# Splitting two table loads and moving the issue of the first feed-forward weights and of the inverse tables

## Chip, core and metric

The kernel runs on one core of a Trainium2 chip. The metric is the device time of one execution in microseconds (us): the median of several runs, with a profile taken of one further execution. Five engines work side by side, each through its own list of instructions in order: PE (matmuls), DVE and ACT (elementwise work, and moving results out of PSUM, the matmul accumulators), POOL, and SP (SyncE), which here only issues DMA transfers. PEld is PE's loading of stationary operands. The transfers of SP and of POOL run on the same 16 DMA engines.

## What is computed

A token mixer in the frequency domain, then a feed-forward block, each after a layer norm and with a residual. S is 2048, D is 576, F is 4608, all in bf16.

```python
def _A_ref(x, w_r, w_i):
    X = rfft2(x.astype(float32), axes=(-2, -1))
    X = X * (w_r + 1j * w_i)
    return irfft2(X, s=(S, D), axes=(-2, -1)).astype(bfloat16)

def _B_ref(x, w_gate, w_up, w_down):
    return (_gelu(x @ w_gate) * (x @ w_up)) @ w_down

x = A_x
h = x + _A_ref(_layernorm(x), A_w_r, A_w_i)
h2 = h + _B_ref(_layernorm(h), B_w_gate, B_w_up, B_w_down)
```

## The kernel before

The 2048 rows are held as 16 chunks of 128. The transforms are matmuls with constant tables that lie in DRAM and are loaded by DMA. The work goes through four stages.

1. **First layer norm and transform** (to about 20 us). Chunks of x and the table ATAB are loaded, the rows are scaled, and matmuls of line 551 give the tile U.
2. **Filter stage** (about 20 to 44 us). It runs over 16 groups of frequencies, numbered 0 to 15 in the order of GORD (group index 1 to 15, then 0). For each group there are five kinds of step. `D` (line 640) transforms along D with the table FT, its two halves written `D` and `d`, and is evicted to CUS. `B` (line 660) is a forward transform of 16 points with the table BT, evicted to YS. `T` (line 673, on DVE) multiplies by the filter weights WS. `V` and `v` (line 681) are the two halves of the inverse 16-point transform of the first 256 columns, with the table VT, evicted to V. `R` and `r` (line 698) do the same for the last 32 columns of four groups at once, with VT too; their result RB is scattered to VR by small DMAs (line 242, the helper that issues every DMA).
3. **Inverse stage** (about 44 to 57 us). `I`, `i` (line 830, with the table DT) and `N`, `o` (line 847, with the table IT) finish the inverse transform of eight of the chunks. `E` evicts to GS, `a` adds the residual, `s`, `q`, `c`, `n` are the second layer norm, `u` and `U` (line 899, with the unit matrix IDT) turn the normed rows, and `e` evicts them to the tile HT. The other eight chunks are done later, between the first feed-forward matmuls, with the tables DP and ITD (from about 63 us).
4. **Feed-forward** (from 57 us to the end). `G0` and `G1` are its first matmuls (line 939): G0 covers the first 256 of the first 512 rows, G1 the others. They use weight slot 0 of the tile WG. Line 1039 is the down projection.

The order inside the filter and the inverse stage is written out by hand, in the strings `SEQF` and `SEQ`. The part of `SEQF` around the first steps of `V` and `R` reads

```python
... d8 D7 T3 B4 d7 V0 D6 v0 V1 T5 d6 v1 R0 V2 r0 v2 T4 ...
```

Semaphore waits are derived from names: an operation lists what it reads and writes, and the engine that issues it waits for the last writers. A DMA is issued in the order of the program on its engine. Where SP must not issue a DMA too early, `hold()` makes SP wait for the last PE operation emitted so far.

Two lists of loads matter here. The first is issued by SP at the start with no waits: x and ATAB, FT (432 KB), BT (128 KB), the first half of the filter weights WS (groups 1 to 8), VT (384 KB), the second half of WS, and the two small rows of group 0 (`w_zero`). Once the weights are there, half of WS is copied to the other partitions, by POOL, DVE and POOL's DMAs (`dup_w`).

The second is the dictionary `LOADS`. Its keys are steps of `SEQF`, or of `SEQ` with a dot in front. After that step is emitted, the loads named in its value are: `0` to `9` are ten pieces of the first feed-forward weights (`wg0_part`, gate and up columns 0 to 1151 into slot 0 of WG, eight of 288 KB and two of 144 KB, each behind a `hold()`), `t` is `tab_load` (DT, IT and the unit matrix, behind a wait for the last copy of WS), and `d` is `tab2_load` (DP and ITD, behind a `hold()`). Piece 9 completes the tile; the matmuls of line 939 wait for all ten.

BT holds two tables of 64 KB: `BT[:, 0]` serves the fifteen groups with nonzero index, `BT[:, 1]` group index 0, which comes last (B15). VT holds six of 64 KB: `VT[:, 0]` serves the `V` steps of the fifteen groups, 1 and 2 those of group index 0 (V15), 3 to 5 the `R` steps.

Of the kernel before, what the change touches and what calls it, by code (L numbers as in the profile page):

```python
# [27 lines left out]
SEQF = """D2 D0 d2 D1 d0 d1 B2 D5 B0 d5 T2 D3 B1 d3 D4 T0 T1 B5 d4 D8 B3 d8 D7 T3 B4 d7 V0 D6 v0 V1 T5 d6 v1 R0 V2 r0 v2 T4 B6 D9 B8 T6 V3 d9 D11 v3 d11 B7 D10 B9 d10 V6 V4 T7 v6 v4 V5 B10 v5 R1 D12 T8 r1 d12 B11 T9 V7 D14 v7 T10 d14 D13 B12 d13 D15 T11 V9 T12 d15 v9 V8 B13 v8 R2 r2 T13 B14 T14 B15 V12 V10 v12 v10 V13 V11 T15 v13 V14 v11 v14 V15 R3 v15 r3""".split()  # L28
VENG = [('act',), ('act', 'dve'), ('act', 'dve'), ('act', 'dve'), ('act', 'dve'), ('dve',), ('act', 'dve'), ('act', 'dve'), ('dve',), ('act', 'dve'), ('act',), ('dve',), ('act',), ('act', 'dve'), ('act',), ('act', 'dve')]
DENG, BENG = ['act', 'dve', 'act', 'act', 'act', 'act', 'act', 'act', 'dve', 'act', 'act', 'act', 'act', 'act', 'act', 'act'], ['act', 'dve', 'act', 'act', 'act', 'act', 'act', 'dve', 'act', 'act', 'act', 'act', 'act', 'act', 'act', 'act']  # L30
LOADS = {"r0": "t", "v12": "0", "v15": "1", ".I0": "2", ".i1": "3", ".N0": "4", ".i3": "5", ".o1": "6", ".N3": "7", ".o3": "8 9", ".i7": "d"}
RENG = ['dve', 'act', 'act', 'act', 'act']
QR = ((0, 1), (1, 2), (2, 3), (3, 4), (4, 8), (8, 16))
DEF0, DSTEP = 3, 4
# [3 lines left out]
def _np_bf16(a):  # L38
    npdt = mybir.dt.np(BF16)
    return np.ascontiguousarray(np.asarray(a, dtype=np.float32).astype(npdt))  # L40
# [291 lines left out]
def _build(nc, A_x, A_w_r, A_w_i, B_w_gate, B_w_up, B_w_down, out):  # L332
    P = Prog(nc)
    T = build_tables()
    dram = {n: nc.inline_tensor(_np_bf16(T[n]), name="c_" + n.lower()) for n in T}
    PE, DVE, ACT, SP, POOL = "pe", "dve", "act", "sp", "pool"
# [51 lines left out]
    FT = sb.alloc("FT", [128, 6, 2 * HK], BF16)  # L388
    BT = sb.alloc("BT", [128, 2, 2, 128], BF16)
    VT = sb.alloc("VT", [128, 6, 2, 128], BF16)  # L390
# [20 lines left out]
    TR = sb.alloc("TR", [128, 2, 2, 2, 128], BF16)  # L411
# [9 lines left out]
    PS = nc.alloc_psum_tensor("PS", [128, 4096], F32)  # L421

    def bank(b, p0=0, p1=128, c0=0, c1=512):
        return PS[p0:p1, b * 512 + c0:b * 512 + c1]

    def banks(b, n, w):
        return PS[:, b * 512:(b + n) * 512].rearrange("p (a c) -> p a c", a=n)[:, :, 0:w]
# [16 lines left out]
    for i, w in enumerate(LORD):  # L444
        (x_load if w[0] == "x" else atb_load)(i, int(w[1:].split("-")[0]), int(w.split("-")[1]))
    P.dma(SP, FT[:, :, :].rearrange("p a b -> p (a b)"), dram["FTAB"][:, :], "ft", w=["FT"])
    P.dma(SP, BT[:, :, :, :].rearrange("p a b c -> p (a b c)"), dram["BTAB"][:, :], "bt", w=["BT"])

    def w_up(pl, hf):
        g0, g1 = ((0, 9), (9, 16))[hf]  # L450
# [5 lines left out]
    def w_down(pl, hf, sls=(0, 1, 2, 3), eng=SP, sem=""):  # L456
        g0, g1 = ((1, 9), (9, 16))[hf]
        src = (A_w_r, A_w_i)[pl].tensor
        for sl in sls:
            p0 = 64 * (sl // 2) + 32  # L460
            P.dma(eng, WS[p0 + sl % 2:p0 + 32:2, sl // 2, pl, g0:g1, :], bass.AP(src, (64 + 16 * (3 - sl) + 16 - g0) * K2, [[128 * K2, 16], [-K2, g1 - g0], [1, K2]]),
                  f"w{pl}{hf}{sem}", w=[("W", hf, pl, 2 + sl)])

    def w_zero(pl):
        for jp in range(2):
            P.dma(SP, WS[64 * jp + 32:64 * jp + 64, jp, pl, 0, :], bass.AP((A_w_r, A_w_i)[pl].tensor, (64 + 32 * jp) * K2, [[128 * K2, 16], [(-16 if jp else 48) * K2, 2], [1, K2]]),
                  f"wz{pl}", w=[("W", 2, pl, jp)])

    for pl in (1, 0):
        w_up(pl, 0)  # L470
        w_down(pl, 0)
    P.dma(SP, VT[:, :, :, :].rearrange("p a b c -> p (a b c)"), dram["VTAB"][:, :], "vt", w=["VT"])
    for pl in (1, 0):
        w_up(pl, 1)
        w_down(pl, 1, (0, 1, 2, 3) if pl else (0, 1))
    for pl in (1, 0):
        w_zero(pl)
    GORD = list(range(1, NG)) + [0]
    wkeys = [[("W", hf, pl, h) for pl in range(2) for h in range(6 if hf < 2 else 2)] for hf in range(3)]

# [100 lines left out]
    for w in SEQ1:  # L581
        a = w[1:]
# [9 lines left out]
    for t, w in enumerate(SEQF):  # L592
        k, i = w[0], w[1:].rstrip("abc")
        if k in "DBVR":
            b = min((b for b in used if b not in busy), key=lambda b: used[b])
# [4 lines left out]
        elif k in "dvr":  # L600
            b = FB[k.upper(), int(i)]
# [3 lines left out]
    def ev(eng, dst, src, r, w):  # L605
        fn = (lambda v: v.tensor_copy(dst, src)) if eng == DVE else (lambda a: a.activation(dst, src, ACTF.Copy))  # L606
        P.op(eng, fn, r=r, w=w)
# [47 lines left out]
    def st_B(i, eng=ACT):  # L655
        sl, s3, sp_ = i % NY, i % 3, 1 if GORD[i] == 0 else 0
        b0 = FB["B", i]
        for m in range(2):
            for h in range(2):
                P.op(PE, lambda t, m=m, h=h: t.matmul(bank(b0 + h, 0, 128, 0, KW), BT[64 * h:64 * h + 64, sp_, m, :], CUS[64 * h:64 * h + 64, s3, m, :], start=(m == 0), stop=(m == 1)),  # L660
                     r=[("CU", s3), "BT"], w=[("PS", b0 + h)])
        ev(eng, YS[:, sl, :, :], banks(b0, 2, KW), [("PS", b0), ("PS", b0 + 1)], [("Y", sl)])

    def st_T(i, hs=(0, 1)):
        g, sl, z = GORD[i], i % NY, i % NZ
        q, j = i // 4 % 2, i % 4
# [9 lines left out]
    def st_V(i, second, engs):  # L676
        g, z, b0 = GORD[i], i % NZ, FB["V", i]

        def mm(h, o, ct, first, last, after):
            c, t_ = ct  # L680
            return P.op(PE, lambda t: t.matmul(bank(b0 + o, 0, 128, 128 * c, 128 * c + 128), TP[64 * h:64 * h + 64, z, o, t_, c:256:2], VT[64 * h:64 * h + 64, 0 if g else 1 + o, t_, :],  # L681
                                               start=first, stop=last), r=[("T", z), "VT"], w=[("PS", b0 + o)], after=after)

        halves(("V", i), second, [[(c, t_) for c in range(2) for t_ in range(2)]] * 2, mm)
        if not second:
            return
        v5 = V[:, :, :, :, g, :, :].rearrange("p c t n j e -> p j (c t n) e")
        n = 2 // len(engs)
        for a, e in enumerate(engs):
            ev(e, v5[:, n * a:n * a + n], banks(b0 + a, n, 256).rearrange("p a (c e) -> p a c e", e=4), [("PS", b0 + a + k) for k in range(n)], [("V", g, a + k) for k in range(n)])  # L690

    def st_R(q, second):
        js = range(4 * q, 4 * q + 4)
        b0 = FB["R", q]

        def mm(h, o, pt, first, last, after):
            part, t_ = pt
            return P.op(PE, lambda t: t.matmul(bank(b0 + o, 0, 128, 128 * part, 128 * part + 128), TR[64 * h:64 * h + 64, q % 2, o, t_, :], VT[64 * h:64 * h + 64, 4 + o if part else 3, t_, :], start=first, stop=last),  # L698
                        r=[("TR", q % 2, j) for j in range(4)] + ["VT"], w=[("PS", b0 + o)], after=after)

        halves(("R", q), second, [[(part, t_) for part in range(1 + (q == 3)) for t_ in range(2)]] * 2, mm)
        if not second:
            return
        keys = [("PS", b0), ("PS", b0 + 1)]
        if q < 3:
            ev(RENG[q], RB[:, q, :, :, :, :].rearrange("p t o e n -> p o t (e n)"), banks(b0, 2, 128).rearrange("p o (t x) -> p o t x", t=2), keys, [("RB", q)])
            for j, i in enumerate(js):
                for t_ in range(2):
                    k = (2 * j + t_) % 3 > 0
                    P.dma((SP, POOL)[k], VR[64 * t_ + 32 * (j % 2):64 * t_ + 32 * (j % 2) + 32, GORD[i], :, :, :], RB[32 * j:32 * j + 32, q, t_, :, :, :], f"r{q}{k:d}", r=[("RB", q)], w=[("V", GORD[i], 2 + t_)])  # L710
            return
        for i in js:
            j, g = i % 4, GORD[i]
            for t_ in range(2):
                dst = VR[64 * t_ + 32 * (j % 2):64 * t_ + 32 * (j % 2) + 32, g, :, :, :].rearrange("p o e n -> p o (e n)")
                src = PS[32 * j:32 * j + 32, b0 * 512:(b0 + 2) * 512].rearrange("p (a c) -> p a c", a=2)[:, :, 128 * (i == LAST) + 64 * t_:128 * (i == LAST) + 64 * t_ + 64]
                ev((ACT, DVE, DVE, ACT)[j], dst, src, keys, [("V", g, 2 + t_)])
# [21 lines left out]
    c = 0  # L739
    while c < NT:  # L740
        c1 = c + 1
        while c not in ACT_TILES and c1 < NT and c1 not in ACT_TILES:
# [3 lines left out]
             r=[(keys, k) for k in range(c, c1)], w=[("NM", k) for k in range(c, c1)])  # L746
        c = c1
    for k in (2, 3):
        for jp in range(2):
            last = dup_w(k, jp)  # L750
# [22 lines left out]
    def loads(w):  # L773
        for v in LOADS.get(w, "").split():
            (tab_load if v == "t" else tab2_load if v == "d" else lambda: wg0_part(int(v)))()

    for w in SEQF:
        i = int(w[1:].rstrip("abc"))
# [14 lines left out]


    P.alias(sum(wkeys, []) + sum(dup, []), [("WG", j, k) for j in (1, 2) for k in range(4)])
    P.alias(["FT", "BT", "VT"], [("HT", 0, i, k) for i in range(4) for k in range(5)])

    vmain = [("V", g, c) for g in range(NG) for c in range(2)]
    vtail = [("V", g, c) for g in range(NG) for c in range(2, 4)]
# [4 lines left out]
    SLOT, last, held, ing = {}, [sorted(used.values()).index(used[2 * b]) - 4 for b in range(4)], set(), False  # L804
    for t, w in enumerate(SEQ):
        k, i = w[0], int(w[1:].rstrip("ADSP"))
        if k in "INu":
            b = min((b for b in range(2 * ing, 4) if b not in held), key=lambda b: last[b])
# [3 lines left out]
        elif k in "ioUEae":  # L812
            b = SLOT[{"i": "I", "o": "N", "U": "u", "E": "I", "a": "N", "e": "u"}[k], i] // 2
# [145 lines left out]
    for w in SEQ:  # L959
        a = w[1:]  # L960
# [96 lines left out]
    for tb in range(4):  # L1057
# [26 lines left out]
        for w in "0 1 0 2 1 3 2 3".split() if tb < 3 else "0 1 0 2 1 2".split():  # L1084
            first = ("Z", tb, int(w)) not in ends
# [39 lines left out]
```

## Time and profile before

| what | value |
| --- | --- |
| median of 3 runs | 489.72 us (488.74 to 489.88) |
| profiled execution | 487.7 us, span of its instructions 485.9 us |
| granted TensorE clock | 1.00 |
| PE busy | 476.7 us, 98% of the span |
| DVE, ACT, POOL busy | 182.9, 146.6, 52.8 us |
| chain that ended last | PE 93%, DMA 1% |
| matmuls of line 939 with slot WG | 2142, 233.3 us busy |
| DMA moved | 33.19 MB, 68 GB/s over the span |

The profile is that of one execution on the chip. Times in its rows are microseconds from the start of the span. A timeline row gives start, duration, engine, line, operation, what is written and read, and in brackets how long the engine stood idle before it and what ended that. A row of waits gives the engine and line that waited, what it waited for, and then the total in us, the number of times and the longest. A windows row gives the stretch, its length, the busy time of the engine with its instruction count, the granted clock, the mean busy share of the 16 DMA engines (which can pass 1 where transfers overlap in one engine), and GB/s. SP's own instructions appear as SPq.

### The profile page before, as it was taken

Reading aid. Unit: us, or ns where it says so; the run is one execution under the profiler, and the core shown is the slowest. Engines: PE = TensorE matmul, PEld = TensorE weight load, DVE = VectorE, ACT = ScalarE, POOL = GpSimd, SP = SyncE. Lnnn points to the kernel's source line nnn. Section 1 sums busy time; section 2 is a strip of 40 time slices with the busy share of each in tenths; the row PEclk is TensorE's granted clock in tenths of the full one; section 3 lists DMA queues with packets and bytes.
Section 4 is the critical chain, followed back from the end, with each engine's and each line's share of the span. In section 5 each row is a group of like instructions: output and inputs, shape, how many; then the busy total and the mean of one; then the engine's idle time right before and its main releaser. Section 6 shows DMA issues by size and latency. Waiting matters only on the chain.

```text
span 485.9 us, 12883 instructions
## 1 busy us (share of the span) xinstructions
PE 476.7 (98%) x5872; PEld 279.4 (57%) x5872; DVE 182.9 (38%) x366; ACT 146.6 (30%) x295; POOL 52.8 (11%) x88
## 2 busy tenths in 40 slices
PE   7899899999999999999999999999999999999998
PEld 3777665544477744444577644444777444444774
DVE  7898756566501133333200233333101233333011
ACT  6998664443400023322200023322100133223000
POOL 6873317010120000000000000000000000000000
PEclk9999999999999999999999999999999999999999
DMA  8965598941440001100000011000000000000000
GB/s 287 210 161 177 175 306 285 377 110 24 131 143 26 27 15 20 23 0 1 1 15 15 26 21 23 14 2 1 3 13 26 14 1 0 1 1 1 3 26 26
DMA packets 26966, 33.19 MB, mean 68 GB/s; under 512 B 12560, under 2 KB 19104, under 8 KB 26912
## 3 DMA queue, kind: packets, MB, share of 16 engines
q1 hardware_dynamic: 23248, 19.87, 14.7%
q0 software_dynamic: 3664, 12.50, 8.0%
q8 instruction: 46, 0.75, 0.7%
q14 instruction: 8, 0.07, 0.0%
HBM read 26.21 MB, written 2.36 MB: 59 GB/s over the span
## 4 chain that ended last, share of the span: by engine, by line
PE 93%; DMA 1%; DVE 0%; issue 0%; SPq 0%; DVEq 0%
PE PS L939 58%; PE PS L1039 27%; PE PS L1051 2%; PE PS L640 2%; PE PS L681 2%; DMA WG<-in_B_w_up_dram 1%; PE PS L830 1%; PE PS L660 1%; PE PS L989 1%; PE PS L847 1%; PE PS L1006 0%; PE PS L698 0%; DVE CUS L606 0%; DVE V L606 0%; SPq L242 0%
## 5 line engine op out<-in xcount | busy, mean ns | idle before, releaser
L939 PE MATMUL PS<-HT,WG 64*128 64x512 bf16 (+1 forms) x2142 | 233.3, 372 | 1.2 <-DMA WG<-in_B_w_up_dram 1.2
L939 PEld LDWEIGHTS PS<-HT,WG 64*128 64x128 bf16 x2142 | 105.2, 94 | 116.1 <-DMA WG<-in_B_w_up_dram 1.3
L947 ACT ACTIVATE GL<-PS 128x512 bf16<-128x512 f32 x144 | 85.7, 596 | 282.9 <-PE PS L939 282.9
L948 DVE TENSOR_TENSOR AT<-GL,PS 128x512 bf16<-128x512 bf16 x144 | 98.8, 687 | 167.1 <-ACT GL L947 167.1
L1039 PE MATMUL PS<-WD,AT 64*128 64x288 bf16 x2160 | 132.9, 283 | 0.0
L1039 PEld LDWEIGHTS PS<-WD,AT 64*128 64x128 bf16 x2160 | 103.3, 94 | 29.8
L1026 DVE TENSOR_TENSOR OS<-PS,XO 128x288 bf16<-128x288 f32 (+2 forms) x32 | 13.3, 453 | 125.5 <-PE PS L1039 118.0
L939 PE MATMUL PS<-HT,WGX 64*128 64x512 bf16 x486 | 53.4, 376 | 0.0
L939 PEld LDWEIGHTS PS<-HT,WGX 64*128 64x128 bf16 x486 | 23.2, 94 | 29.2
L856 ACT ACTIVATE OS<-XO,NM 128x576 bf16<-128x576 bf16 x15 | 11.6, 774 | 11.4 <-DVE XO L1010 11.4
L640 PE MATMUL PS<-FT,U 64*128 64x288 bf16 x160 | 13.5, 284 | 0.3 <-DVE CUS L606 0.3
L673 DVE TENSOR_TENSOR TP<-YS,WS 128x1024 bf16<-128x1024 bf16 x16 | 11.0, 688 | 0.5 <-DMA WS<-WS 0.5
L551 PE MATMUL PS<-ATS,XO 128*128 128x128 bf16 x96 | 8.2, 219 | 3.0 <-POOL ATS L520 2.1
L494 DVE BATCH_NORM_STATS2 ST<-XO 128x6 f32<-128x288 bf16 x26 | 9.9, 441 | 2.1 <-DMA XO<-in_A_x_dram 2.0
L562 ACT ACTIVATE U<-PS 128x384 bf16<-128x384 f32 (+2 forms) x31 | 10.4, 419 | 1.1 <-PE PS L551 0.9
L681 PE MATMUL PS<-VT,TP 64*128 64x128 bf16 x256 | 10.0, 217 | 0.0
L242 POOL DMA_DIRECT2D WG<-in_B_w_gate_dram x9 | 6.1, 678 | 35.1 <-DMA WG<-in_B_w_gate_dram 30.6
L551 PEld LDWEIGHTS PS<-ATS,XO 128*128 128x128 bf16 x96 | 6.9, 98 | 4.4 <-POOL ATS L520 2.9
L242 POOL DMA_DIRECT2D WD<-in_B_w_down_dram x9 | 6.7, 755 | 24.4 <-PE PS L1006 24.4
L606 ACT ACTIVATE CUS<-PS 128x576 bf16<-128x576 f32 x14 | 9.0, 653 | 0.8 <-PE PS L640 0.7
L1051 PE MATMUL PS<-WD,AT 128*128 128x448 bf16 (+1 forms) x72 | 9.0, 286 | 0.0
L606 ACT ACTIVATE YS<-PS 128x576 bf16<-128x576 f32 x14 | 8.8, 653 | 0.2
(88 smaller groups left out, 229.5 us busy)
## 6 DMA issues: line engine op xcount, KB each, us to landing
WD<-in_B_w_down_dram POOLq DMA_DIRECT2D x9, 576.0 KB, 10.6
WG<-in_B_w_up_dram SPq DMA_DIRECT2D x6, 576.0 KB, 6.8
WG<-in_B_w_gate_dram POOLq DMA_DIRECT2D x6, 576.0 KB, 5.8
out_dram<-OS SPq DMA_DIRECT2D x30, 72.0 KB, 1.7
XO<-in_A_x_dram SPq DMA_DIRECT2D x3, 576.0 KB, 7.5
WG<-in_B_w_gate_dram SPq DMA_DIRECT2D x4, 288.0 KB, 3.8
WG<-in_B_w_up_dram SPq DMA_DIRECT2D x4, 288.0 KB, 3.6
WGX<-in_B_w_up_dram SPq DMA_DIRECT2D x2, 576.0 KB, 4.6
```

The lines of the kernel that those rows point to most:

```text
L242: fn = lambda e: e.dma_start(out_ap, in_ap)
L551: P.op(PE, lambda t, b=b, lhs=lhs, p0=p0, p1=p1, s=s, e=e, o=o, c=c: t.matmul(bank(b, p0, p1, o, o + 128), lhs, ATS[:, c, :], start=s, sto ...
L606: fn = (lambda v: v.tensor_copy(dst, src)) if eng == DVE else (lambda a: a.activation(dst, src, ACTF.Copy))
L640: return P.op(PE, lambda t: t.matmul(bank(b0 + o, 0, 128, 0, 2 * HK), U[64 * h:64 * h + 64, us, 2 * i:2 * i + 2, :, :], FT[64 * h:64 * h + ...
L681: return P.op(PE, lambda t: t.matmul(bank(b0 + o, 0, 128, 128 * c, 128 * c + 128), TP[64 * h:64 * h + 64, z, o, t_, c:256:2], VT[64 * h:64 ...
L856: P.op(ACT, lambda a, c=c, out=out: a.activation(out, XO[:, c, 0:D], ACTF.Square, bias=NM[:, c:c + 1], accum_out=SB2[:, 1, c:c + 1]), r=[( ...
L939: op = P.op(PE, lambda t, h0=h0, kt=kt, wt=wt, b=b, s=(not second and j == 0), e=(second and j == n - 1): t.matmul(bank(b, 0, 128, c0, c1) ...
L947: P.op(ACT, lambda a: a.activation(GL[:, s2, :], bank(b0), ACTF.Gelu_apprx_tanh), r=[("PS", b0)], w=[("GL", s2)])
L948: P.op(DVE, lambda v: v.tensor_tensor(AT[:, f, :], GL[:, s2, :], bank(b0 + 1), op=ALU.mult), r=[("GL", s2), ("PS", b0 + 1)], w=[("AT", f)])
L1026: P.op(DVE, lambda v: v.tensor_tensor(OS[:, p % 2, d0:d1], bank(b, 0, 128, 0, d1 - d0), XO[:, c, d0:d1], op=ALU.add), r=[("PS", b), ("X", ...
L1039: e[h] = P.op(PE, lambda t, f=f, h=h, r0=r0, j=j: t.matmul(bank(b0 + h, 0, 128, 0, 288), AT[r0:r0 + 64, f, 128 * p:128 * p + 128], WD[r0:r ...
L1051: P.op(PE, lambda t, b=b, d0=d0, d1=d1, f=f, j=j: t.matmul(bank(b, 0, 128, 0, d1 - d0), AT[:, f, 128 * p:128 * p + 128], WD[:, f, d0:d1], ...
```

## The change

Three things are changed, and no computation.

- The loads of the two 16-point tables are each made in two parts. `BT[:, 0]` and `VT[:, 0]` (64 KB each) stay where the whole table was loaded. `VT[:, 1:6]` (320 KB) and `BT[:, 1]` (64 KB) are issued after the last of the filter weights, under the names VT2 and BT2. B15 now waits for BT2, and V15 and all `R` steps for VT2.
- The ten weight pieces are attached to other steps: 0 and 1 to d7, 2 to v9, 3 to v8, 4 to v12, 5 to v13, 6 to v15, 7 to I0, 8 and 9 to i1. Before, the first was attached to v12 and the last to o3 of the inverse stage.
- `tab_load` moves from r0 to r1, and `tab2_load` from i7 to N1.

```diff
-LOADS = {"r0": "t", "v12": "0", "v15": "1", ".I0": "2", ".i1": "3", ".N0": "4", ".i3": "5", ".o1": "6", ".N3": "7", ".o3": "8 9", ".i7": "d"}
+LOADS = {"d7": "0 1", "r1": "t", "v9": "2", "v8": "3", "v12": "4", "v13": "5", "v15": "6", ".I0": "7", ".i1": "8 9", ".N1": "d"}
...
-    P.dma(SP, BT[:, :, :, :].rearrange("p a b c -> p (a b c)"), dram["BTAB"][:, :], "bt", w=["BT"])
+    P.dma(SP, BT[:, 0, :, :].rearrange("p b c -> p (b c)"), dram["BTAB"][:, 0:256], "bt", w=["BT"])
...
-    P.dma(SP, VT[:, :, :, :].rearrange("p a b c -> p (a b c)"), dram["VTAB"][:, :], "vt", w=["VT"])
+    P.dma(SP, VT[:, 0, :, :].rearrange("p b c -> p (b c)"), dram["VTAB"][:, 0:256], "vt", w=["VT"])
     for pl in (1, 0):
         w_up(pl, 1)
         w_down(pl, 1, (0, 1, 2, 3) if pl else (0, 1))
     for pl in (1, 0):
         w_zero(pl)
+    P.dma(SP, VT[:, 1:6, :, :].rearrange("p a b c -> p (a b c)"), dram["VTAB"][:, 256:1536], "vt2", w=["VT2"])
+    P.dma(SP, BT[:, 1, :, :].rearrange("p b c -> p (b c)"), dram["BTAB"][:, 256:512], "bt2", w=["BT2"])
...
 st_B:  r=[("CU", s3), "BT2" if sp_ else "BT"]
 st_V:  r=[("T", z), "VT" if g else "VT2"]
 st_R:  r=[("TR", q % 2, j) for j in range(4)] + ["VT2"]
```

The last three lines give only what the reading side of each step now names.

More of the change, by code (lines that the diff above doesn't have):

```diff
@@ L660, in st_B @@
                 P.op(PE, lambda t, m=m, h=h: t.matmul(bank(b0 + h, 0, 128, 0, KW), BT[64 * h:64 * h + 64, sp_, m, :], CUS[64 * h:64 * h + 64, s3, m, :], start=(m == 0), stop=(m == 1)),
-                     r=[("CU", s3), "BT"], w=[("PS", b0 + h)])
+                     r=[("CU", s3), "BT2" if sp_ else "BT"], w=[("PS", b0 + h)])
         ev(eng, YS[:, sl, :, :], banks(b0, 2, KW), [("PS", b0), ("PS", b0 + 1)], [("Y", sl)])
@@ L681, in mm @@
             return P.op(PE, lambda t: t.matmul(bank(b0 + o, 0, 128, 128 * c, 128 * c + 128), TP[64 * h:64 * h + 64, z, o, t_, c:256:2], VT[64 * h:64 * h + 64, 0 if g else 1 + o, t_, :],
-                                               start=first, stop=last), r=[("T", z), "VT"], w=[("PS", b0 + o)], after=after)
+                                               start=first, stop=last), r=[("T", z), "VT" if g else "VT2"], w=[("PS", b0 + o)], after=after)
         halves(("V", i), second, [[(c, t_) for c in range(2) for t_ in range(2)]] * 2, mm)
@@ L698, in mm @@
             return P.op(PE, lambda t: t.matmul(bank(b0 + o, 0, 128, 128 * part, 128 * part + 128), TR[64 * h:64 * h + 64, q % 2, o, t_, :], VT[64 * h:64 * h + 64, 4 + o if part else 3, t_, :], start=first, stop=last),
-                        r=[("TR", q % 2, j) for j in range(4)] + ["VT"], w=[("PS", b0 + o)], after=after)
+                        r=[("TR", q % 2, j) for j in range(4)] + ["VT2"], w=[("PS", b0 + o)], after=after)
         halves(("R", q), second, [[(part, t_) for part in range(1 + (q == 3)) for t_ in range(2)]] * 2, mm)
@@ L795, in _build @@
     P.alias(sum(wkeys, []) + sum(dup, []), [("WG", j, k) for j in (1, 2) for k in range(4)])
-    P.alias(["FT", "BT", "VT"], [("HT", 0, i, k) for i in range(4) for k in range(5)])
+    P.alias(["FT", "BT", "VT", "BT2", "VT2"], [("HT", 0, i, k) for i in range(4) for k in range(5)])
     vmain = [("V", g, c) for g in range(NG) for c in range(2)]
```

## The prediction

> **What bounds the kernel now.** I read the page first: PE is busy 476.7 of the 485.9 us of the span and the chain of waits gives it 93%. So the change can only matter where PE stands still between 20 us, where the tables of the change are first used, and the first feed-forward matmul. The view of PE's waits from 20 to 57.5 us has four rows in all:
>
> ```profile
> PE PS L939 <- DMA WG<-in_B_w_up_dram: 1.2, 1, 1.2
> PE PS L830 <- DVE V L606: 0.4, 1, 0.4
> PE PS L640 <- DVE CUS L606: 0.3, 1, 0.3
> PE PS L830 <- DVE XO L853: 0.2, 1, 0.2
> ```
>
> That is 2.1 us to be had. The first row is the last of the ten weight pieces. The chain of waits up to 60 us, and SyncE's part of the timeline, show how it comes about:
>
> ```profile
> 51.15 0.37 PE PS L830 x6
> 51.52 0.27 PE PS L847 x4
> 51.78 0.39 SPq L242
> 52.17 0.04 issue
> 52.22 4.96 DMA WG<-in_B_w_up_dram
> 57.17 0.05 issue
> 57.22 2.79 PE PS L939 x47
> ```
>
> ```profile
> 14.05 0.59 SPq L242 DMA_DIRECT2D VT<-c_vtab  x1
> ...
> 22.96 1.36 SPq L242 DMA_DIRECT2D WS<-in_A_w_r_dram  x2
> 30.20 2.65 SPq L242 DMA_DIRECT2D VR<-RB  x3
> 37.55 0.33 SPq L242 DMA_DIRECT2D DT<-c_dtab  x1
> ...
> 43.43 0.58 SPq L242 DMA_DIRECT2D WG<-in_B_w_gate_dram  x1
> ...
> 52.22 0.60 SPq L242 DMA_DIRECT2D WG<-in_B_w_up_dram  x1
> ```
>
> The reader is to see that the pieces start only at 43.43, that the last is issued at 52.22 because it is held to an inverse matmul that ends at 51.78, and that it lands 4.96 us later, since the pieces and the deferred tables keep the transfer engines about 0.9 busy from 45 to 55 us. Meanwhile the stretches from 27 us on stand almost empty. The windows by microsecond (PE busy, clock, DMA share, GB/s) read:
>
> ```profile
> 25.00:26.00 1.00, 1.00 (x20) 1.00 0.88 213
> 26.00:27.00 1.00, 1.00 (x20) 1.00 0.74 198
> 27.00:28.00 1.00, 1.00 (x27) 1.00 0.21 59
> 28.00:29.00 1.00, 1.00 (x36) 1.00 0.04 10
> 29.00:30.00 1.00, 1.00 (x34) 1.00 0.00 0
> ```
>
> **Part 1, the weight pieces.** The change issues the same ten DMAs, only earlier. Their holds now end, by the places of these steps in PE's chain: d7 at 27.5 us (pieces 0 and 1), v9 and v8 at 39.2 and 39.9 (2, 3), v12, v13 and v15 between 41.6 and 44.0 (4, 5, 6), I0 at 44.8 (7), i1 at about 46.5 (8, 9). The last piece is therefore issued by about 47.4, and with the slowest landing of such a piece here (4.96 us) it is there at 52.4, some 3.7 us before it can be used. What is late next at G0, line 939? The timeline around it:
>
> ```profile
> 54.64 1.38 ACT L606 ACTIVATE HT<-PS 128x640 bf16<-128x640 f32 x2
> 55.84 0.22 PE L899 MATMUL PS<-IDT,HN 64*128 64x64 bf16 x4
> 57.21 0.99 PEld L939 LDWEIGHTS PS<-HT,WG 64*128 64x128 bf16 x20 [1.28 <-DMA WG<-in_B_w_up_dram]
> 57.22 1.16 PE L939 MATMUL PS<-HT,WG 64*128 64x256 bf16 x18 [1.16 <-DMA WG<-in_B_w_up_dram]
> ```
>
> The tile HT of chunk 0 is evicted at 54.64 + 1.38 = 56.02, PE's own last matmul ends at 56.06. G0's four PSUM banks were freed by the same evictions. HT of chunk 3 comes at 57.53, but is first read by G1, 36 matmuls of 69 ns (6.33 us for 92) after G0 starts, at about 58.6. So G0 can start at about 56.10: **1.12 us gained** of the 1.16; the rest is the step from an eviction to PE.
>
> On SyncE each piece is 0.33 to 0.58 us of issue. Pieces 0 and 1 (27.5 to 28.5) stand ahead of the scatter of RB for R0, which waits until 30.2 anyway. Pieces 2 and 3 stand ahead of the scatter of R2 (issued from 40.76, when RB is evicted) and are issued by 40.4. Their 576 KB do lie ahead of that scatter in the queue: DT, IT, EYE and both pieces are 1480 KB, 4.5 us at the 318 to 363 GB/s of 39 to 41 us, so the scatter moves from about 43.6 on and lands near 45.2, as now. It is read at 45.74, after an eviction that ends at 45.60. I take nothing and keep 0 to 0.5 us. On the same engines, pieces 0 and 1 fall into the empty stretch from 28.5 to 30.5, before the copies of WS that POOL issues at 29.69. If these came later, T8 on DVE (35.55) would be the first to wait, and its V step on PE follows more than 2 us later: nothing.
>
> **Part 2, the inverse tables.** DT, IT and EYE go from r0 to r1. That frees R1's scatter on SyncE, which now stands behind a wait that ends at 37.54, and puts its three issues (2.0 us from 35.9) ahead of DT. DT is issued near 38.0, 0.45 us later, and lands 3.0 us on, at 41; PE wants it at 44.52. IT takes 4.3 and is wanted at 46.70. Nothing, with 3 us of cover. DP and ITD move from i7 to N1, ahead of their use at 63.3: nothing.
>
> **Part 3, the first half of BT.** BT shrinks from 128 to 64 KB ahead of the WS loads. The 0.3 us wait on CUS is a chain from those: DVE idles 0.89 us for the last of w_r, copies it, and only then evicts the CUS that PE waits for.
>
> ```profile
> 22.04 1.07 DVE L728 COPY WS<-WS 64x1444 bf16<-64x1444 bf16 x2 [0.89 <-DMA WS<-in_A_w_r_dram]
> 23.03 0.75 DVE L606 CAST CUS<-PS 128x576 bf16<-128x576 f32 x1
> ```
>
> From the issue rows FT lands at 4.80 + 10.6 = 15.4 and BT at 5.55 + 10.4 = 16.0, so on the engine that is last BT takes 0.55 us; half of it, with descriptors of half the size, saves 0.15 to 0.28. I take **0.22 us gained** (bounds 0 and 0.30, the whole wait).
>
> **Part 4, the second part of VT, a new wait.** VT2 (320 KB) now follows the last WS load and so is issued at 24.4 us, BT2 at 25.0. R0, the first step to read VT2, runs on PE now at 28.92, by part 3 at 28.7. PE is in order, so whatever R0 waits, all behind it waits (V2, r0, and the whole filter, which runs on PE without a gap until 43.96). When does VT2 land? The change moves bytes and adds none, so the transfers end when they end now: the windows show the engines busy to 27 us, and by fifths of a microsecond the last share (0.07) is that of 28.2 to 28.4, so that the last movement ends at 28.4. The DMAs nearest to it are the last WS load, issued at 23.60 and landed 5.3 us later at 28.9, and POOL's, issued at 24.4 with 4.7, at 29.1. BT2 stands behind VT2 and takes some 0.3 of that tail. So VT2 lands between 28.5 and 29.1, and R0 waits 0 to 0.4: I take **0.2 us lost**. The bounds are wider: 0 if the WS loads, no longer behind 384 KB of tables, clear the tail early, and 5.4 us if it takes the 9.7 us that VT takes now (24.4 + 9.7 = 34.1).
>
> The Trainium skill's page DMA: Bandwidth & Descriptors speaks against this part, in Anatomy of one DMA: it puts a fixed 2.0 us on each transfer, most of it the receipt after the last byte. The trace has 0.7 us from the last movement (28.4) to the last landing (29.1), and so disagrees. By the page VT2 would be there at 30.4, and the sum would be +0.4 us.
>
> BT2 is used by B15 at 40.3: nothing. T5's wait of 0.47 us on DVE for a copy of WS lies beside PE work.
>
> **The sum.** -1.12 - 0.22 + 0.20 = -1.14 us. The profiled execution took 487.7 (span 485.9 and 1.8 around it), so it would take 486.6; the median of the runs, 489.72, lies 2.0 above that execution, and I carry the difference over: 488.6. All after G0 shifts as a block, since PE is busy 10.00 of every 10 us from 60 on. About 0.3%, 1.47 us, is what a measurement of this kernel can tell from no change; the three runs spread by 1.14.
>
> **The rivals.** (A) The forecast, 0.40; with the spread of the runs about 0.12 of it would show as a gain over 0.3%. (B) More: VT2 is there before R0, the CUS wait goes entirely, and steps of the inverse stage that PE spends on "issue" (0.3 us in the chain from 44 to 57) shrink with the emptier engines: 1.12 + 0.30 + 0.3 = 1.7, 488.0. For it: WS loads are rid of 384 KB ahead of them. Against: no row proves that "issue" is due to transfers. 0.34, of which 0.30 beyond 0.3%. (C) Cancelled: VT2 takes the 6.6 us from issue to landing of the last four w_i loads (63 KB each, issued from 15.9 on), so it lands at 31.0 and R0 waits 2.3: -1.34 + 2.3 = +1.0, 490.7. For it: those are the nearest loads with a full queue; against: the loads nearest in time took 5.3 and 4.7. 0.12. (The page's 30.4 would lie between A and C.) (D) Slower: VT2 is served as VT is now, 9.7 us after its issue. R0 waits 5.4 us, the sum is +4.1, 493.8. It decides once VT2 lands past 28.7 + 1.34 + 1.47 = 31.5. For it: the row of VT. Against: the queue behind which VT waited is empty by 28.4. 0.12. (E) The pieces are early and G0 waits as before, because SyncE is held up at DT's wait: 0.02, no change.
>
> **How the numbers follow.** Faster: 0.12 + 0.30 = 0.42. Slower: D, 0.12. Within: the rest, 0.46. The range takes A, B and C: 487.7 (B less 0.3 of the runs' spread) to 490.7 (C). A's own is 488.2 to 489.2.
>
> **What would show it.** Right: no row of PE waiting at L939, G0 at about 56.1, the last piece landed by 52.4; a PE wait at L698 of 0.2 us for VT2; the CUS wait below 0.15. Part 4 is wrong if L698's row is above 0.6 us, or is missing; part 1 if a row at L939 stays, then naming ACT or DVE instead of a DMA. The whole is wrong if PE's four rows together do not fall by about 1.1 us.

## The result and the profile after

The changed kernel is slower: a median of 490.81 us in 20 runs (488.36 to 495.03) against 488.50 for the kernel before in 20 runs beside it (487.32 to 490.38). The ratio of the runs is 1.005, with a 95% interval of 1.0028 to 1.0073. The profiled execution took 493.51 us, its span is 491.7 us, and its mean granted clock is 0.993. Below, a stand of PE is a stretch in which it idles.

PE's waits from 20 to 62 us in the changed kernel (engine and line that waited, what for, total us, times, longest). Two lines were added to the file, so that 939 is now 941, 830 is 832, 698 is 700:

```profile
PE PS L832 <- DMA VR<-RB: 3.5, 1, 3.5
PE PS L553 <- DVE ATS L527: 0.8, 1, 0.8
PE PS L832 <- DVE V L608: 0.4, 1, 0.4
PE PS L832 <- DVE XO L855: 0.2, 1, 0.2
```

The wait for the weight pieces is gone, and so is the one on CUS. A new one of 3.5 us stands in the first row: the inverse stage waits for the last columns, which the small DMAs carry from RB to VR. The chain of waits there, in order of time:

```profile
43.04 1.74 POOL VR L242 x4
44.78 0.21 issue
44.99 5.89 DMA VR<-RB
50.88 0.35 issue
51.23 1.90 PE PS L832 x14
```

That DMA moves 8 KB and takes 5.89 us to land. SP's timeline shows what had been issued ahead of it and beside it:

```profile
29.65 0.33 SPq L242 DMA_DIRECT2D WG<-in_B_w_gate_dram  x1
30.02 0.43 SPq L242 DMA_DIRECT2D WG<-in_B_w_up_dram  x1
32.17 8.34 SPq L242 DMA_DIRECT2D VR<-RB  x6
40.55 0.58 SPq L242 DMA_DIRECT2D DT<-c_dtab  x1
41.18 0.44 SPq L242 DMA_DIRECT2D IT<-c_itab  x1
41.66 0.43 SPq L242 DMA_DIRECT2D IDT<-c_eye  x1
42.13 0.43 SPq L242 DMA_DIRECT2D WG<-in_B_w_gate_dram  x1
42.61 0.43 SPq L242 DMA_DIRECT2D WG<-in_B_w_up_dram  x1
43.08 1.78 SPq L242 DMA_DIRECT2D VR<-RB  x3
```

The reader is to see five bulk transfers (DT, IT, the unit matrix, pieces 2 and 3: 1480 KB) issued in the 2.5 us right ahead of the scatter of R2. In the kernel before, the scatter stood ahead of all pieces, and DT was issued 3.2 us before it (37.55 and 40.76).

The second loss is in the clock. The windows by microsecond (PE busy, clock, DMA share, GB/s) around the end of that wait:

```profile
50.00:51.00 1.00, 0.00 (x0) 0.97 0.25 88
51.00:52.00 1.00, 0.77 (x8) 0.50 0.09 35
52.00:53.00 1.00, 1.00 (x12) 0.50 0.04 14
53.00:54.00 1.00, 1.00 (x12) 0.50 0.30 56
54.00:55.00 1.00, 1.00 (x18) 0.82 0.69 212
```

From 50.95 us, just before the stand ends, the granted clock is halved for 3.4 us, and matmuls of the same form take 0.71 us for four at 51.46 and 0.42 at 54.97:

```profile
51.23 0.46 PE L832 MATMUL PS<-DT,VR 64*128 64x288 bf16 x2 [3.49 <-DMA VR<-RB]
51.46 0.71 PE L832 MATMUL PS<-DT,V 64*128 64x288 bf16 x4
...
54.97 0.42 PE L832 MATMUL PS<-DT,V 64*128 64x288 bf16 x4
```

This execution has a second such fall from 13.4 us on, after PE's stand of 1.95 us at line 553. The stand is in the kernel before too (2.06 us, with no fall in its profile). That fall and a slower front move everything after it by some 2.1 us, which is why the times above are later than those the prediction names.

A run with one fall has a mean clock of 0.996 or 0.997, with two 0.993, with three 0.990, so the runs can be sorted by it:

| kernel | runs at clock 1.000 | their mean | mean with one fall | falls a run |
| --- | --- | --- | --- | --- |
| before (beside the first four experiments) | 24 of 35 | 487.79 | 489.24 | 0.31 |
| changed | 6 of 20 | 488.81 | 490.79 | 1.10 |

At full clock the change costs 1.0 us. It also has 0.8 more falls a run: they lift the mean of all its runs 2.25 us above that at full clock, and that of the kernel before 0.45. Together this is 2.8 us, where the means of the 20 and 20 runs differ by 2.5 (491.06 and 488.60) and the medians by 2.3.

### The profile page after: what moved, and what is told of

Its sections match the earlier page's. It is cut to its first block, busy times and chain, and to the rows that moved or that the text cites. A ratio compares the mean times of both kernels' runs of the same rounds, so it can differ in the third digit from the quotient of the medians.

```text
span 491.7 us, 12886 instructions
## 1 busy us (share of the span) xinstructions
PE 480.3 (98%) x5872; PEld 282.8 (58%) x5872; DVE 184.6 (38%) x366; ACT 146.9 (30%) x295; POOL 51.8 (11%) x88
## 4 chain that ended last, share of the span: by engine, by line
PE 92%; DMA 3%; DVE 1%; ACT 1%; POOL 1%; issue 0%; SPq 0%; POOLq 0%; DVEq 0%
PE PS L941 57%; PE PS L1041 27%; PE PS L1053 2%; PE PS L642 2%; DMA XO<-in_A_x_dram 2%; DMA VR<-RB 1%; PE PS L553 1%; PE PS L683 1%; PE PS L832 1%; PE PS L991 1%; DVE XO L855 1%; PE PS L662 1%; ACT U L564 0%; PE PS L849 0%; SPq L242 0%
## 5 line engine op out<-in xcount | busy, mean ns | idle before, releaser
L553 PE MATMUL PS<-ATS,XO 128*128 128x128 bf16 x96 | 9.7, 238 | 2.8 <-POOL ATS L522 1.9
L553 PEld LDWEIGHTS PS<-ATS,XO 128*128 128x128 bf16 x96 | 7.9, 108 | 4.2 <-POOL ATS L522 2.4
L553 PE MATMUL PS<-ATS,XN 128*128 128x128 bf16 x64 | 8.6, 238 | 0.3 <-ACT U L564 0.3
```

The costliest lines, as they stand in the source:

```text
L553: P.op(PE, lambda t, b=b, lhs=lhs, p0=p0, p1=p1, s=s, e=e, o=o, c=c: t.matmul(bank(b, p0, p1, o, o + 128), lhs, ATS[:, c, :], start=s, sto ...
```

## The experiments

Each was timed against the kernel before on the same chip. Ratios have their 95% intervals; one that holds 1 leaves the sign open.

**Which part.** Theory 1: the bulk ahead of and beside R2's scatter. Theory 2: the split of the tables. Theory 3: the move of the inverse tables from r0 to r1.

Only the split:

```diff
-LOADS = {"d7": "0 1", "r1": "t", "v9": "2", ...}
+LOADS = {"r0": "t", "v12": "0", "v15": "1", ...}   # as before
```

> The tables in two parts as in the changed kernel, all issue places of pieces and inverse tables as before. Theory 1 (the pieces and the inverse tables now stand ahead of the scatter of R2 into VR and share the engines with POOL's part of it, so that the first VR matmul of the inverse stage waits): no wait for VR, the wait of 1.2 us for the pieces at the first feed-forward matmul is back, time within 0.5 us of the kernel before. Theory 2 (the split of the tables costs the time): about 2 us slower than before.

Measured: 487.99 us against 488.09, ratio 0.9991 (0.9972 to 1.0011). PE's longest waits:

```profile
PE PS L941 <- DVE HT L608: 1.5, 1, 1.5
PE PS L832 <- DVE V L608: 0.4, 1, 0.4
PE PS L700 <- DMA VT<-c_vtab: 0.3, 1, 0.3
```

No wait for VR; the stand at line 941 is back. The row names DVE, but the last piece, issued at 52.98 there, landed at 58.27, and PE goes on at 58.32. The split is cleared.

Only the new places:

```diff
-    P.dma(SP, BT[:, 0, ...], dram["BTAB"][:, 0:256], "bt", w=["BT"])   # and VT, VT2, BT2
+    P.dma(SP, BT[:, :, ...], dram["BTAB"][:, :], "bt", w=["BT"])       # whole tables, as before
```

> The tables whole as before, all issue places as in the changed kernel. Theory 1: like the changed kernel, a wait of 2 to 4 us for VR at the first VR matmul, no wait for the pieces, about 2 us slower than before. Theory 2: about 1.1 us faster than before, since only the wait for the pieces is gone.

Measured: 490.46 us, ratio 1.0051 (1.0027 to 1.0075), a wait of 2.5 us for VR. The loss is there with the new places alone. At clock 1.000 the mean is 489.03, 1.24 above before, close to the wait of 2.46 less the 1.16 saved at the weights (1.30).

Pieces 2 to 9 behind R2's scatter:

```diff
-LOADS = {... "r1": "t", "v9": "2", "v8": "3", "v12": "4", "v13": "5", "v15": "6", ".I0": "7", ".i1": "8 9", ".N1": "d"}
+LOADS = {... "r1": "t", "v12": "2", "v15": "3", ".I0": "4", ".i1": "5", ".N0": "6", ".i3": "7", ".o1": "8 9", ".N3": "d"}
```

> The changed kernel, but only pieces 0 and 1 stay early (at d7); 2 to 9 go to v12, v15, I0, i1, N0, i3 and o1, so that none is issued by SyncE ahead of the scatter of R2; DP and ITD to N3. Theory 1, if the pieces are what is in the way: wait for VR at most 0.5 us, no wait for the pieces, 0.8 to 1.3 us faster than before. Theory 2: still 1 us or more slower than before. Theory 3 (DT, IT and EYE, moved from r0 to r1, are what is in the way): a wait for VR of 2 us or more stays, as slow as the changed kernel.

Measured: 487.06 us, 1.0 below before, ratio 0.9983 (0.9962 to 1.0003); the wait for VR is 0.4 us, there is none for the pieces. The pieces are the larger share of the wait.

The inverse tables back at r0:

```diff
-LOADS = {"d7": "0 1", "r1": "t", "v9": "2", ...}
+LOADS = {"d7": "0 1", "r0": "t", "v9": "2", ...}
```

> The changed kernel, but DT, IT and EYE are back at r0, ahead of the scatter of R1; the pieces stay as changed. Theory 3: no wait for VR, about 1 us faster than before. Theory 1 (pieces): the wait for VR stays, if shorter, 1 to 3 us; 0.5 to 2 us slower than before.

Measured: 488.29 us, ratio 1.0014 (0.9991 to 1.0036).

```profile
PE PS L832 <- DMA VR<-RB: 1.5, 1, 1.5
PE PS L832 <- DVE V L608: 0.4, 1, 0.4
PE PS L832 <- DVE XO L855: 0.2, 1, 0.2
```

The wait is shorter but stays; the time is only 0.2 us above before, less than the 0.5 to 2 expected. So tables and pieces add up: 1480 KB close ahead of the scatter give 2.4 to 3.5 us, the two pieces with DT issued 4.3 us before the scatter (36.96 and 41.22) 1.5, the tables alone 0.4.

**Which pieces.** Those issued ahead of the scatter (2, 3), or those beside it (4 to 6)?

```diff
-... "v9": "2", "v8": "3", "v12": "4", ...
+... "r2": "2 3", "v12": "4", ...
```

> The changed kernel, but pieces 2 and 3 go to r2, behind SyncE's part of the scatter of R2; pieces 4 to 6 stay at v12, v13, v15 and the inverse tables at r1. Theory 1a (bytes that SyncE puts ahead of the scatter are what is late): wait for VR at most 0.6 us, 0.5 to 1.2 us faster than before. Theory 1b (pieces 4 to 6 beside the scatter are what is in the way): a wait of 1.5 us or more stays, 0.5 us or more slower than before.

Measured: 487.02 us, ratio 0.9986 (0.9966 to 1.0005), no wait for VR:

```profile
PE PS L832 <- DVE V L608: 0.4, 1, 0.4
PE PS L662 <- ACT YS L608: 0.2, 1, 0.2
PE PS L832 <- DVE XO L855: 0.2, 1, 0.2
```

The mirror, with 4 to 9 from i0 on and 2 and 3 where the change put them:

```diff
-... "v9": "2", "v8": "3", "v12": "4", "v13": "5", "v15": "6", ".I0": "7", ".i1": "8 9", ".N1": "d"}
+... "v9": "2", "v8": "3", ".i0": "4 5", ".i1": "6 7", ".N0": "8 9", ".N3": "d"}
```

> The mirror: the changed kernel with pieces 2 and 3 at v9 and v8 and the tables at r1, so that both stand ahead of the scatter of R2, but pieces 4 to 9 only from i0 on, after the VR matmul that waits. Theory 1a: the wait for VR stays, 1.5 to 3.5 us, 0.5 to 2.5 us slower than before. Theory 1b: wait at most 0.6 us, about 1 us faster than before.

Measured: 490.43 us, ratio 1.0056 (1.0034 to 1.0078), a wait of 2.4 us for VR. That settles it: with the tables at r1, it is the two pieces that bring the wait, issued from 39.88 in the mirror and from 43.44 in the run before it; pieces 4 to 9 do not. The scatter itself is issued at nearly the same time in both (SP from 40.84 and 40.57, POOL from 40.87 and 40.83), so the delay lies between issue and landing. The rows of the issues in the 2.5 us of R2's scatter (count, size, median us from issue to landing), first with pieces 2 and 3 behind it, then in the mirror:

```profile
VR<-RB POOLq DMA_DIRECT2D x5, 8.0 KB, 1.9
VR<-RB SPq DMA_DIRECT2D x3, 8.0 KB, 3.3
```

```profile
VR<-RB POOLq DMA_DIRECT2D x5, 8.0 KB, 3.9
VR<-RB SPq DMA_DIRECT2D x3, 8.0 KB, 4.2
```

POOL's DMAs go through another queue and are held up more than SP's own, by these medians.

**The clock.** Theory 4: a stand of PE now and then halves the clock for 3.4 us, and this is the rest of the loss. Ten matmuls that compute nothing used, in the place of the wait:

```diff
+        if w == "i0":
+            for _ in range(10):
+                P.op(PE, matmul(bank(6), ZD[:, 0:128], ZD[:, :]), r=["ZD"], w=[("PS", 6)])
```

> The changed kernel with ten matmuls of the zero tile (about 2.2 us of PE at full clock) put into PE's order ahead of the first VR matmul, where the wait stands; they compute nothing that is used. Theory 4 (part of the loss is the granted clock, which halves for 3.4 us after a long stand of PE, 2 us a time): the wait left is 0 to 1.5 us, runs with a clock below 1.000 fall from 14 of 20 to the share of the kernel before (11 of 35), median about 489, 1.5 us below the changed kernel. Rival (the loss is the wait alone): the clock is as it was and the median stays at 490.5 to 491.

Measured: 490.90 us, ratio 1.0060 (1.0035 to 1.0084), 3 of 6 runs below clock 1.000. The median missed by nearly 2 us. It left the front's stand open, and the fillers and what follows them end later than VR lands, 48.3 us, so that they seem to cost about 0.9 us themselves (489.68 at full clock, three runs, against 488.81). This run decided nothing, so each stand was filled by itself and both together:

```diff
-SEQ1 = """... k202 ..."""
+SEQ1 = """... k209 ..."""   # seven more zero matmuls near 11 us
```

> The changed kernel with the same seven matmuls in the stand near 11 us, so that the wait for VR is the only long stand left. Theory 4: runs below 1.000 remain, at most one fall of 3.4 us in each (0.3 to 0.8 a run, from 1.1), median 1 to 2.5 us slower than before. Rival (the falls all come from the front): no run below 1.000, about 1 us slower than before.

Measured: 490.39 us, ratio 1.0046 (1.0026 to 1.0066), 5 of 8 runs below 1.000, 0.75 falls a run; one run has two falls, where at most one was expected. In its profile the wait for VR (2.4 us) is followed by two windows of half clock in a row (windows of 2 us, columns as above):

```profile
46.00:48.00 2.00, 0.00 (x0) 0.83 0.89 295
48.00:50.00 2.00, 1.72 (x16) 0.50 0.17 65
50.00:52.00 2.00, 2.00 (x20) 0.50 0.48 127
52.00:54.00 2.00, 2.00 (x20) 0.50 0.19 43
54.00:56.00 2.00, 1.94 (x31) 0.97 0.66 228
```

With both fillers, the two diffs together:

> The changed kernel with both fillers, seven matmuls near 11 us and ten ahead of the first VR matmul. Theory 4: no run below 1.000; the wait stays in another form, so that it is 1 to 2 us slower than before at full clock. Rival: runs below 1.000 as in the changed kernel.

Measured: 489.27 us, ratio 1.0026 (1.0013 to 1.0039), all 12 runs at 1.000, where the changed kernel had 6 of 20. At full clock it is 1.5 us above before (489.36 against 487.82). Theory 4 holds: it takes both stands to explain the changed kernel's falls, and with the front filled it is the wait for VR that brings them (5 of 8 runs with it, none of 12 with it filled).

**Versions without the collision.** Pieces 2 to 9 late and the tables at r0:

```diff
-LOADS = {"d7": "0 1", "r1": "t", "v9": "2", ...}
+LOADS = {"d7": "0 1", "r0": "t", "v12": "2", "v15": "3", ".I0": "4", ".i1": "5", ".N0": "6", ".i3": "7", ".o1": "8 9", ".N3": "d"}
```

> The kernel with pieces 2 to 9 late (from v12 on) and, besides, DT, IT and EYE back at r0. Theory 1a: nothing of size stands ahead of the scatter of R2, no wait for VR, 0.8 to 1.5 us faster than before, and 0 to 0.4 us faster than with the tables at r1. Rival (the tables at r0 hold up the scatter of R1 behind the wait for the copies of WS, and that now comes last): a wait for VR of 0.5 us or more.

Measured: 487.15 us against 488.08, ratio 0.9982 (0.9965 to 0.9999), no wait for VR or the pieces, 6 of 6 runs at full clock. It does not differ from the tables at r1 by more than the runs spread.

The same places with BT and VT whole:

> The places of loads of the kernel with pieces 2 to 9 late and the inverse tables at r0, but BT and VT loaded whole as before. If the split is neutral: no wait at VR or at the first feed-forward matmul, 0.6 to 1.3 us faster than before, within 0.3 us of the same with the split. If the split carries part of that gain: only 0 to 0.5 us faster than before.

Measured: 486.91 us against 488.26, ratio 0.9977 (0.9958 to 0.9996). The split brings nothing that shows. Its profile has a wait of 0.5 us for VR, which had been expected to be none.

The split version with the front filled:

> The kernel with the split, pieces 2 to 9 late and the inverse tables at r0, and seven more matmuls of the zero tile (1.5 us) in PE's stand of 2 us near 11 us. Theory 4 (a stand of PE now and then halves the clock for 3.4 us): no long stand is left before the end, no run below a clock of 1.000, 0.8 to 1.6 us faster than before. Rival (the fillers push the first transform back, or the clock falls without a stand): not faster than without them, or runs below 1.000 remain.

Measured: 486.82 us against 488.26, ratio 0.9981 (0.9961 to 1.0002), 11 of 12 runs at 1.000; one run, with a fall, took 491.76, so that falls are not gone (11 of 31 runs of the kernel before had one). The five versions without the wait, or with at most 0.5 us of it, lie 0.9 to 1.4 us under the kernel before and cannot be told from one another; the intervals of two of them stay below 1, those of three just reach it.

## Why the prediction was wrong

**The step that failed** is in part 1, the sentence on the scatter of R2: "lands near 45.2, as now ... I take nothing and keep 0 to 0.5 us". In the profile of the kernel with the new places alone, where the clock stays full, the issue times came out as predicted: DT at 37.87 (38.0 forecast), the scatter from 40.58 (40.76). The landing did not: SP's last at 47.29, POOL's at 47.61, where 45.5 was needed. The chain of waits there names POOL's:

```profile
42.80 4.82 DMA VR<-RB
47.61 0.35 issue
47.96 1.08 PE PS L830 x14
```

Two things were wrong in that step. The prediction put the end of the 1480 KB at 43.6, by a mean rate, and the scatter's landing 1.6 us behind that. The rate about held (windows of half a microsecond add up to 1.45 MB moved from 38.0 to 43.5), but piece 3 landed only at 45.02, 1.4 us after the mean rate had the bytes through, and the last of the small DMAs came 2.3 and 2.6 us behind that instead of 1.6. And POOL's five DMAs, which landed last, were not costed at all. Measured, the wait is 2.4 to 3.5 us where nothing was taken, against the 1.12 saved.

**Its second half**, the clock, was not in the prediction: it priced a PE wait at its length. A wait of about 2.4 us also brought a fall of the clock in 5 of 8 runs where it was the only long stand. A run of the changed kernel with one fall was 2.0 us longer than one without (490.79 against 488.81), one of the kernel before 1.45. The profile of before has the clock at 1.00, which showed that such stands need not do it, not that they cannot.

**The slower rivals** named VT2's landing (part 4) as their place. Part 4 held to within 0.7 us: VT2 landed 4.9 us after its issue at 24.50 in the changed kernel's profile, at 29.4, and at 27.8 to 29.7 in the ten others with the split (28.5 to 29.1 forecast). R0's wait was 0.2 to 0.5 us in four of those ten (0.2 forecast) and none in the rest. Its row is missing from the changed kernel's profile, which the prediction had named as a sign against part 4; but R0 ran there only at 31.04, since the front was 2.1 us late, so that this profile doesn't test it. By the Trainium skill, DMA: Bandwidth & Descriptors (Anatomy of one DMA), VT2 should have come near 30.4; the rows put it 0.7 us earlier or more. That section fits its 2.0 us to DMAs that GpSimd issues, and VT2 is issued by SP. The slower side was right in kind, a DMA that PE waits for, and stood at the wrong tile.

**Part 1's gain was right.** Without the collision the first feed-forward matmul starts right behind PE's last one, at 56.02 with pieces 2 and 3 behind the scatter and at 56.14 with pieces 2 to 9 late and the tables at r0 (56.10 forecast):

```profile
55.74 0.22 PE L901 MATMUL PS<-IDT,HN 64*128 64x64 bf16 x4
56.02 2.25 PE L941 MATMUL PS<-HT,WG 64*128 64x256 bf16 x38
```

The kernels without the collision are 0.9 to 1.4 us faster; the forecast sum was 1.14, of which 1.12 is this part. That the sum comes out so near is in part luck, since parts 3 and 4 cancel in it and neither is clear of the noise.

**Part 3 is not shown.** The wait on CUS is absent from the changed kernel, but also where the tables are whole and only the places are new, and the split alone gained 0.2 us at full clock (487.56 against 487.79), less than the runs can tell.

**Part 2** (the tables at r1) was called free with 3 us of cover for DT and IT. Their own use was covered. Their 904 KB stood ahead of R2's scatter in the kernel before too, 3.2 us ahead; with the new places it was 2.7 (37.87 and 40.58), with the pieces close behind them. PE waits 2.5 us there, and 1.5 with the tables at r0, 4.3 us ahead.

## What to carry to other kernels

Ahead of each small DMA that an engine will wait for, count the bytes issued on all queues in the few microseconds before it, not only those of its own queue, and price its landing from rows taken behind full engines. Prefetch belongs behind such a DMA if the prefetch has slack: here 576 KB moved behind the scatter by 3.6 us turned a loss of 2.3 us into 1.1 us less than before. And a wait of 1.5 us or more on PE is to be priced above its length, since the granted clock can fall after it.

## What the runs showed of the hardware

- The clock falls by half in windows of 3.41 us (50.9 to 54.4 us and 13.4 to 16.8 in the changed kernel's profile) or two of them together, after stands of PE that need not be that long: it fell after stands of 1.5 us (split only), 1.8 (tables whole, pieces late), 1.95, 2.4 and 3.5, and did not after others of 1.5, 2.06 and 2.46. The falls of one execution lie on a grid: they begin 37.55 us apart in the changed kernel's profile, 11 times 3.413, and 440.3 in the mirror's (48.70 and, after the last matmul, 489.01), 129 times 3.413. The windows of that grid, cut at its edges, show in part why the same stand does and does not bring a fall. First the two windows right before the changed kernel's falls; then the two over the stand of 2.46 us (new places only, grid from the fall at 487.10 after the last matmul), which an edge at 46.78 cuts in half:

```profile
9.98:13.40 3.42, 1.19 (x13) 1.00 1.06 328
47.53:50.95 3.42, 0.21 (x4) 1.00 0.76 269
```

```profile
43.37:46.78 3.41, 1.79 (x39) 1.00 0.95 289
46.78:50.19 3.41, 2.23 (x36) 1.00 0.41 133
```

  The stand of 2.06 us in the kernel before is cut likewise (2.49 and 2.14 us busy, no fall). In the profiles here five falls from full clock came after windows with PE busy for 0.2 to 1.6 us, and none after others of 1.6 to 2.5. A sixth came after 1.9 (split only), so busy time alone does not draw the line. The Trainium skill's TensorE: Matmul & The Clock Gate (What's actually happening) gives the same 3413 ns and calls the window free-running; the whole multiples agree. Its rule of thumb that only gaps above about 3.4 us matter (HAM oscillation) does not hold here.
- Small DMAs on POOL's queue went from 1.9 to 3.9 us, issue to landing, when 576 KB more were queued on SP's ahead of them. The Trainium skill's DMA: Bandwidth & Descriptors (Issuing engines are not separate DMA queues) says that all run on the same 16 engines and interleave; the 2 us are what that cost here.
